# Transposing q by DMA in f16 halves instead of by TensorE in float32

## The chip, the cores and the metric

The kernel runs on one core of a Trainium2 chip. The metric is the device time of one execution in microseconds, the median of several runs. Where runs are compared, the kernel before and the changed one run on the same chip.

## The reference

Eight batches of eight heads, 576 tokens, head size 64: a linear attention, and a feed-forward layer on its output.

```python
# q, k, v: [8, 8, 576, 64] float32; w_in [512, 2048], w_out [2048, 512]
q_s = exp(q - max(q, -1));  q_s = q_s / (sum(q_s, -1) + 1e-9)
k_s = exp(k - max(k, 2));   k_s = k_s / (sum(k_s, 2) + 1e-9)
kv  = einsum('bhsd,bhse->bhde', k_s, v)
x   = einsum('bhsd,bhde->bhse', q_s, kv)     # heads side by side: [4608, 512]
h   = x @ w_in
g   = h * erf(softplus(h))
out = g @ w_out                              # [4608, 512] float32
```

## The kernel before

The feed-forward layer runs over twelve blocks of 384 tokens (three to a pair of batches), each in four groups of 512 hidden columns: 48 items, n = 0 to 47. From item 4 on, matmuls are in f16 with each float32 operand split into a high and a low half, and three products stand for one (high by high, high by low, low by high). For item n, `mm1(n, k)` makes the hidden values in the PSUM banks pX, pY and pZ (a scheme with seven products of halves, k = 0 to 3; groups of twelve matmuls, L905); ScalarE and VectorE copy and add them into the tile H (L917 to L932). `softplus` and `erf` run on ScalarE (L337 is their line, through the helper `act`, and with each goes a table load), `gmul` multiplies on VectorE (L984), and L997 and L1001 split the result into halves. `mm2` multiplies them by w_out into the bank o (L1029, twelve matmuls a group, one group for each 128 tokens), VectorE scales o into ob (L1045), and SP stores it (L1048).

Beside that runs the attention of the batches to come, in the generator `attention(b)`: the k maximum over tokens (`k_max`, L490 to L494, then transposed), q minus its row maximum (L447, L448), exponentials, `kv_mm` and `kv_norm` (kvf is the normalised kv in float32), `kv_split` (from a maximum over all of kv, transposed into x_bk at L119, a scale; then the halves of kv into kvbd, L588 and L589), `q_norm`. Then q, which lies with tokens in rows, is transposed: for a column block c (two heads), `q_cols` puts four transposes of 128 x 128 float32 on TensorE (L610) into a bank qT, and `q_evac` casts it to f16 on ScalarE (L603) and subtracts on VectorE (L604). `x_mm` (L625) makes x from the halves qTs and kvbd, and ScalarE puts it into the blocks of x (L436). The first 512 tokens of a batch are in two tiles q of four heads each (hf = 0, 1; columns 0, 1 and 2, 3); the last 64 of an even batch and its odd partner share the tile qt, transposed (L684) with the odd batch, before the four columns, into qTt and multiplied into xt. Batches 0 and 1 are in float32 throughout.

What sets the order: `pace` takes steps of the generator as the items go on, by the numbers in SHARES, and a scheduler then places every instruction on its engine's queue in that order of priority, as it takes the operands to be ready. Each engine works through its queue in order and waits where an operand isn't there. SP issues the loads and stores in the same way, one queue for all.

The tiles named qT (two buffers) hold the transposed halves; the same two buffers serve `k_max` and kvf.

Of the kernel before, what the change touches and what calls it, by code (L numbers as in the profile page):

```python
# [8 lines left out]
F16 = mybir.dt.float16  # L9
F32 = mybir.dt.float32  # L10
# [3 lines left out]
ALU = mybir.AluOpType  # L14
# [39 lines left out]
def attn_moe_kernel(  # L54
# [15 lines left out]
    TM = 4  # L70
# [26 lines left out]
    vbuf = cp.tile([P, 4, TM, D + 1], F32, name="vbuf")  # L97
    nc.gpsimd.memset(vbuf[:, :, :, D:], 1.0)
    vtail = cp.tile([P, H, D + 1], F32, name="vtail")

    kvbd = []
    for i in range(2):
# [338 lines left out]
    def rows(t):  # L441
        return t.rearrange("p t h d -> p (t h) d")
# [41 lines left out]

    def k_max(b, ks, kt):

        kmax = at.tile([P, H, D], F32, tag="qT", name=f"kmax_{b}")
        k2 = at.tile([P, 2, 4, D], F32, tag="qT", name=f"k2_{b}")
        for hf in range(2):
            nc.vector.tensor_tensor(k2, ks[hf][:, 0:2], ks[hf][:, 2:4], op=ALU.max)  # L490
            nc.vector.tensor_tensor(
                kmax[:, hf * 4:hf * 4 + 4, :], k2[:, 0], k2[:, 1], op=ALU.max
            )
        nc.vector.tensor_tensor(kmax[kt[1]], kmax[kt[1]], kt[0], op=ALU.max)  # L494
        return kmax
# [51 lines left out]
    def kv_norm(b, hf, bk):  # L547
        if b >= E32:
            if hf == 0:
                bat[b]["kvf"] = at.tile([P, NC4, D], F32, tag="qT", name=f"kvf_{b}")  # L550
            kvf = bat[b]["kvf"]
        bkv = bk[:, :2 * W].rearrange("p (c w) -> p c w", c=2)
        rd = at.tile([P, 2, 1], F32, tag="rd", bufs=1, name=f"rd_{b}_{hf}")
        nc.vector.tensor_scalar_add(rd, bkv[:, :, D:], 1e-9)
        nc.vector.reciprocal(rd, rd)
        cs = slice(2 * hf, 2 * hf + 2)
        if b >= E32:
            nc.vector.tensor_tensor(
                kvf[:, cs, :], bkv[:, :, :D], rd.to_broadcast([P, 2, D]), op=ALU.mult
            )  # L560
            return
        for a in range(2):
            ps = slice(a * D, (a + 1) * D)
            nc.vector.tensor_tensor(
                kv32[b][ps, cs, ps], bkv[ps, :, :D], rd[ps].to_broadcast([D, 2, D]),
                op=ALU.mult,
            )
# [25 lines left out]
        if b > 1:  # L593
            nc.vector.tensor_scalar_mul(d["U"], w_u["in"], d["ux"])

    def q_evac(b, bk, name):

        if b < E32:
            qT = at.tile([P, SM], F32, tag="qT", name=name)
            nc.scalar.copy(qT, bk)  # L600
            return qT[:, None, :]
        qT = at.tile([P, 2, SM], F16, tag="qT", name=name)
        nc.scalar.copy(qT[:, 0], bk)  # L603
        nc.vector.tensor_tensor(qT[:, 1], bk, qT[:, 0], op=ALU.subtract)  # L604
        return qT

    def q_cols(b, c, bk):
        hf, c2 = divmod(c, 2)
# [5 lines left out]

    def q_T(b, c, bk):
        q_cols(b, c, bk)
        return q_evac(b, bk, f"qTs_{b}_{c}")

    def x_mm(b, c, out_, qT):

# [15 lines left out]
    def attention(b):  # L636
        d, j, p = bat[b], b % 2, b // 2
        even = bat[b - j]
        tl = slice(j * TAIL, (j + 1) * TAIL)
        ks, qs, kt = d["k"], d["q"], even["kt"][tl]  # L640
        kmax = k_max(b, ks, (kt, tl))
        yield SHARES[0]
        km = k_max_T(b, kmax)
        q_sub(rows(qs[0]), 16, f"q_{b}_0")
        yield SHARES[1]
        kb = k_max_rows(b, km)
        for hf in range(2):
            nc.vector.tensor_tensor(
                ks[hf], ks[hf],
                kb[:, None, hf * 4:hf * 4 + 4, :].to_broadcast([P, TM, 4, D]),  # L650
                op=ALU.subtract,
            )
        nc.vector.tensor_tensor(kt, kt, kb[tl], op=ALU.subtract)
        yield SHARES[2]
        q_sub(rows(qs[1]), 16, f"q_{b}_1")
        if j == 1:
            q_sub(even["qt"], H, f"qt_{p}")
        yield SHARES[3]
        for t in (*ks, kt, qs[0], qs[1], *([even["qt"]] if j == 1 else [])):
            act(t, t, AF.Exp, chain=b > 1)  # L660
        yield SHARES[4]
        kv_norm(b, 0, kv_mm(b, 0))
        d["v"].append(load_half(v, "v", b, 1))
        q_norm(rows(qs[0]), 16, f"q_{b}_0", b)
        yield SHARES[5]
        kv_norm(b, 1, kv_mm(b, 1))
        if b + 1 < B:
            load_kv(b + 1)
        mx = kv_max(b)
        yield SHARES[6]  # L670
        kv_split(b, mx)
        yield SHARES[7]
        q_norm(rows(qs[1]), 16, f"q_{b}_1", b)
        if j == 1:
            q_norm(even["qt"], H, f"qt_{p}", b)
        yield SHARES[8]
        for i in ((3 * p + 1, 3 * p + 2) if j else (3 * p, 3 * p + 1)):
            while not x_free(i):
                yield 0
        if j == 1:  # L680
            qt2 = hd(even["qt"])
            bk = bank(f"qTt_{p}")
            for c in range(NC4):
                nc.tensor.transpose(  # L684
                    bk[:, c * P:(c + 1) * P], qt2[:, c * P:(c + 1) * P], ident
                )
            qT = q_evac(b, bk, f"qTt_{p}")
            if b + 1 < B:
                even_next = bat[b + 1]
                even_next["qt"] = load_tail(q, "qt", p + 1)  # L690
            yield SHARES[9]
            bk = bank(f"xt_{p}")
            x = xblock(p * NBK + 1)
            bk3 = bk.rearrange("p (c s) -> p c s", c=NC4)
            for a in range(2):
                for c in range(NC4):
                    cs = slice(c * P + a * TAIL, c * P + (a + 1) * TAIL)
                    x_mm(2 * p + a, c, bk[:, cs], qT[:, :, cs])
            for a in range(2 if b < E32 else 1):
                w = TAIL if b < E32 else P  # L700
                o = SM - T + a * TAIL
                x_put(
                    bk3[:, :, a * TAIL:a * TAIL + w], x[:, :, o:o + w],
                    bat[a]["sx"] if b < E32 else None,
                )
            yield SHARES[10]
        for c in range(NC4):
            hf, c2 = divmod(c, 2)
            qT = q_T(b, c, bank(f"qT_{b}_{c}"))
            if c2 == 1 and b + 1 < B:  # L710
                load_q(b + 1, hf)
            yield SHARES[11]
            bk = bank(f"x_{b}_{c}")
            x_mm(b, c, bk, qT)
            x_split(b, c, bk)
            if c == NC4 - 1:
                d["xdone"] = True
            yield SHARES[12]
# [14 lines left out]
    def start():  # L733
# [61 lines left out]
        def tc_(c):  # L795
# [3 lines left out]
            if c < 3:  # L799
                bk = psh.tile([P, 512], F32, tag=f"p{'XYZ'[c]}", name=f"qT_0_{c}")  # L800
                qT = r["qT"][:, c]
            else:
                bk = pso.tile([P, 512], F32, tag="o2", name=f"qT_0_{c}")
                qT = at.tile([P, SM], F32, tag="qT", name=f"qTs_0_{c}")
            q_cols(0, c, bk)
            nc.scalar.copy(qT, bk)
            put(f"t{c}", qT[:, None, :])
# [373 lines left out]
```

## Time and profile before

| | |
|---|---|
| three timed runs | 867.26, 867.32, 868.08 us; median 867.32 |
| span of the profiled execution, first to last instruction | 865.1 us (its own time is not recorded apart from the span) |
| TensorE busy | 823.4 us, 95% |
| VectorE busy | 642.5 us, 74% |
| ScalarE busy | 505.9 us, 58% |
| granted TensorE clock, mean | 0.988 |

Matmuls on TensorE overlap, so their busy time is more than the time between their starts. In the rows below, PE is TensorE, PEld its weight loads, DVE is VectorE, ACT is ScalarE, and L12 is line 12 of the kernel. A row of the timeline gives the start in us from the span's start, the length, the engine, the line, the operation, the tiles, how many instructions are merged in it, and the idle time ahead of it with what ended that. A row of the groups gives the count, busy us, the mean ns of one, and the idle us ahead.

### The profile page before, as it was taken

The page shows a single profiled execution, that of the slowest core. Times are in us where ns is not written, and L with a number is a line of the kernel's source. Part 1 is how long each engine was busy: PE and PEld are TensorE (multiplying, and loading weights), DVE is VectorE, ACT ScalarE, POOL GpSimd, SP SyncE. Part 2 cuts the span into 40 slices and gives each one's busy share as a digit, 9 for nine tenths or more (in the row PEclk, how much of TensorE's full clock was granted, in tenths as well). Part 3 has the DMA queues.
Part 4 walks back from the last instruction along what each step waited for, and adds up shares of the span by engine and source line. Part 5 has one row for each costly group of instructions (what it writes and reads, how often), then busy time and mean ns, then how long its engine had stood idle before and what let it go on. Part 6 is the DMA issues. An engine that isn't in the chain of part 4 may idle for free.

```text
span 865.1 us, 15558 instructions
## 1 busy us (share of the span) xinstructions
PE 823.4 (95%) x6556; PEld 570.3 (66%) x6556; DVE 642.5 (74%) x923; ACT 505.9 (58%) x646; POOL 18.2 (2%) x37
## 2 busy tenths in 40 slices
PE   3999996889999999999999999999999999999997
PEld 2655555557766677767776677776776677677672
DVE  6999799899887778858866778867865656653543
ACT  2697677576584567466655467466655456453532
POOL 2101100000000000000000000000000000000000
PEclk9999998889999999999999999999999999999999
DMA  9976730041223202311141212311010000000100
GB/s 270 402 166 184 187 86 1 1 104 26 61 50 80 65 23 50 80 38 25 33 103 32 56 30 50 80 38 25 20 43 2 24 15 1 37 2 1 37 2 37
DMA packets 117381, 55.53 MB, mean 64 GB/s; under 512 B 106560, under 2 KB 108608, under 8 KB 117312
## 3 DMA queue, kind: packets, MB, share of 16 engines
q1 hardware_dynamic: 115136, 46.15, 20.3%
q0 software_dynamic: 2176, 8.39, 2.7%
q8 instruction: 51, 0.84, 0.4%
q14 instruction: 18, 0.15, 0.0%
HBM read 45.09 MB, written 9.44 MB: 63 GB/s over the span
## 4 chain that ended last, share of the span: by engine, by line
PE 73%; DVE 13%; ACT 6%; SPq 3%; DMA 2%; issue 2%; POOL 0%; ACTq 0%; DVEq 0%
PE o L1029 33%; PE pX L905 17%; PE pZ L905 8%; PE pY L905 4%; PE kv L535 3%; ACT L337 2%; ACT G L337 2%; SPq L402 2%; DVE wt L290 2%; PE o L1020 2%; DVE G L984 2%; PE x L625 2%; PE qT L610 1%; DVE H L1001 1%; DMA q<-in_q_dram 1%
## 5 line engine op out<-in xcount | busy, mean ns | idle before, releaser
L1029 PE MATMUL o<-wt,H 128*128 128x512 f16 x1584 | 366.9, 380 | 3.6 <-DVE H L997 3.1
L905 PEld LDWEIGHTS <-wt 128*128 128x128 f16 x3696 | 312.4, 99 | 37.5 <-issue 15.2
L1029 PEld LDWEIGHTS <-H 128*128 128x128 f16 x1584 | 152.4, 98 | 159.0 <-DVE H L997 4.1
L905 PE MATMUL pX<-x,wt 128*128 128x192 f16 x2112 | 208.0, 249 | 9.8 <-ACT H L924 5.7
L337 ACT ACT_TABLE_LOAD x105 | 134.7, 1283 | 7.9 <-DVE H L930 5.7
L984 DVE SCALAR_TENSOR_TENSOR G<-G,small,H 128x1536 f32<-128x1536 f32 x44 | 80.0, 1817 | 65.9 <-ACT G L337 65.8
L905 PE MATMUL pZ<-x,wt 128*128 128x192 f16 x1056 | 103.4, 247 | 0.0
L932 ACT COPY H<-pX 128x384 f32<-128x384 f32 x44 | 20.9, 476 | 139.7 <-PE pX L905 134.7
L337 ACT ACTIVATE G<-H,U 128x768 f32<-128x768 f32 (+1 forms) x60 | 72.8, 1231 | 22.1 <-DVE H L930 21.5
L1001 DVE TENSOR_TENSOR H<-G,H 128x1536 f16<-128x1536 f32 x44 | 77.3, 1756 | 1.1
L337 ACT ACTIVATE G<-G 128x1536 f32<-128x1536 f32 x48 | 71.2, 1484 | 0.5
L905 PE MATMUL pY<-x,wt 128*128 128x192 f16 x528 | 51.1, 246 | 0.5 <-DVE H L917 0.5
L436 ACT ACTIVATE x<-x 128x384 f32<-128x384 f32 (+1 forms) x52 | 17.6, 386 | 56.4 <-PE x L625 54.0
L917 DVE COPY H<-pY 128x384 f32<-128x384 f32 x44 | 24.4, 555 | 30.1 <-PE pY L905 30.1
L997 DVE CAST H<-G 128x1536 f16<-128x1536 f32 x44 | 42.0, 955 | 0.7
L290 DVE SCALAR_TENSOR_TENSOR x<-x,x 128x768 f16<-128x768 f32 (+1 forms) x44 | 37.2, 850 | 5.7 <-ACT x L289 5.6
L289 ACT ACTIVATE x<-x 128x768 f16<-128x768 f32 (+1 forms) x44 | 33.1, 762 | 12.2 <-DVE x L381 12.1
L1045 DVE TENSOR_SCALAR ob<-o,V 128x512 f32<-128x512 f32 x29 | 21.7, 749 | 23.9 <-PE o L1029 23.7
L930 DVE TENSOR_TENSOR H<-pZ,H 128x384 f32<-128x384 f32 x44 | 24.2, 551 | 19.3 <-PE pZ L905 19.3
L919 DVE TENSOR_TENSOR H<-pX,H 128x384 f32<-128x384 f32 x44 | 24.4, 555 | 15.3 <-PE pX L905 14.9
L535 PE MATMUL kv<-vbuf,k 128*64 128x65 f32 x480 | 22.0, 237 | 7.6 <-ACT k L337 5.2
L535 PEld LDWEIGHTS kv<-vbuf,k 128*64 128x64 f32 x480 | 18.7, 149 | 14.5 <-ACT k L337 6.4
(162 smaller groups left out, 823.1 us busy)
## 6 DMA issues: line engine op xcount, KB each, us to landing
out_dram<-ob SPq DMA_DIRECT2D x32, 256.0 KB, 2.2
vbuf<-in_v_dram SPq DMA_DIRECT2D x60, 128.0 KB, 3.0
q<-in_q_dram SPq DMA_DIRECT2D x56, 128.0 KB, 3.0
k<-in_k_dram SPq DMA_DIRECT2D x56, 128.0 KB, 3.3
wt<-in_moe_w_out_dram POOLq DMA_DIRECT2D x5, 1024.0 KB, 6.5
wt<-in_moe_w_in_dram SPq DMA_DIRECT2D x4, 1024.0 KB, 10.7
raw<-in_moe_w_in_dram SPq DMA_DIRECT2D x2, 1024.0 KB, 14.3
wt<-in_moe_w_out_dram SPq DMA_DIRECT2D x2, 1024.0 KB, 16.0
```

The lines of the kernel that those rows point to most:

```text
L289: nc.scalar.activation(hi, src, AF.Copy, scale=s)
L290: nc.vector.scalar_tensor_tensor(lo, src, s, hi, op0=ALU.mult, op1=ALU.subtract)
L337: i = nc.scalar.activation(out_, in_, func, **kw)
L535: nc.tensor.matmul(bk[a * D:(a + 1) * D, c * W:(c + 1) * W], kk, vv, start=(t == 0), stop=(t == TM),)
L905: nc.tensor.matmul(o, w[wl][:, c, a * P:(a + 1) * P], x[:, xl, xi, c, :], start=(new and a == 0 and c == 0 and i == 0), stop=(c == 1 and i ...
L917: nc.vector.tensor_copy(C[0, 0], bank2("Y"))
L919: add(C[0, 0], bank2("X"), C[0, 0], op=ALU.add)
L930: add(C[0, 1], bank2("Z"), C[0, 1], op=ALU.add)
L984: nc.vector.scalar_tensor_tensor(flat(s["G"]), flat(s["G"]), GA[:, g:g + 1], flat(s["H"]), op0=ALU.mult, op1=ALU.mult,)
L997: nc.vector.tensor_copy(flat(s["gh"]), flat(s["G"]))
L1001: nc.vector.tensor_tensor(flat(s["gl"]), flat(s["G"]), flat(s["gh"]), op=ALU.subtract)
L1029: nc.tensor.matmul(o, s[gt][:, a, ts_], w[wl][:, a, :], start=(first_ and a == 0 and i == 0), stop=(last_ and a == FG - 1 and i == 2),)
```

## The change

For batches 2 to 7 the halves are made while q still has tokens in rows: ScalarE casts a whole tile q of 128 x 1024 to f16, VectorE subtracts, both into a scratch tile, and one DMA transpose, issued by SP, puts all sixteen blocks of 128 x 128 into the place where q was. For qt it is eight blocks. `x_mm` reads its operand there. Since q's place is in use until `x_mm` has read it, the loads of the next batch's q and qt stand behind the x products. A single scratch tile asc takes the place of the two buffers named qT: it holds the halves on their way, the k maximum, kvf, and for batches 0 and 1 the transposed q.

```diff
+    asc = cp.tile([P, 2, 512], F32, name="asc")
+    qhl = asc.rearrange("p h n -> p (h n)").bitcast(F16)
...
-        kmax = at.tile([P, H, D], F32, tag="qT", name=f"kmax_{b}")
-        k2 = at.tile([P, 2, 4, D], F32, tag="qT", name=f"k2_{b}")
+        kmax = asc[:, 0].rearrange("p (h d) -> p h d", h=H)
+        k2 = asc[:, 1].rearrange("p (t h d) -> p t h d", t=2, h=4)
...
-                bat[b]["kvf"] = at.tile([P, NC4, D], F32, tag="qT", name=f"kvf_{b}")
+                bat[b]["kvf"] = asc[:, 0, :NC4 * D].rearrange("p (c e) -> p c e", c=NC4)
...
+    def q_halves(q_, n):
+
+        hl = [qhl[:, i * n:(i + 1) * n] for i in range(2)]
+        nc.scalar.copy(hl[0], q_)
+        nc.vector.tensor_tensor(hl[1], q_, hl[0], op=ALU.subtract)
+
+
+    def q_turn(q_, n):
+
+        q_halves(q_, n)
+        t = q_.bitcast(F16).rearrange("p (n s) -> p n s", s=P)
+        nc.sync.dma_start_transpose(t, qhl[:, :2 * n])
+        return t
+
+    def q_turn_half(b, hf):
+        t = q_turn(bat[b]["q"][hf].rearrange("p t h d -> p (t h d)"), TM * 4 * D)
+        t = t.rearrange("p (i t c) s -> p i c t s", i=2, t=TM)
+        for c in range(2):
+            bat[b].setdefault("qT", {})[2 * hf + c] = t[:, :, c]
...
         kv_split(b, mx)
         yield SHARES[7]
+        if b >= E32:
+            q_turn_half(b, 0)
         q_norm(rows(qs[1]), 16, f"q_{b}_1", b)
...
         yield SHARES[8]
+        if b >= E32:
+            q_turn_half(b, 1)
...
+            if b >= E32:
+                qT = q_turn(qt2, H * D).rearrange("p (i c) s -> p i (c s)", i=2)
...
-            if b + 1 < B:
-                even_next = bat[b + 1]
-                even_next["qt"] = load_tail(q, "qt", p + 1)
             yield SHARES[9]
...
+            if b + 1 < B:
+                bat[b + 1]["qt"] = load_tail(q, "qt", p + 1)
             yield SHARES[10]
         for c in range(NC4):
             hf, c2 = divmod(c, 2)
-            qT = q_T(b, c, bank(f"qT_{b}_{c}"))
-            if c2 == 1 and b + 1 < B:
-                load_q(b + 1, hf)
+            qT = q_T(b, c, bank(f"qT_{b}_{c}")) if b < E32 else d["qT"][c]
             yield SHARES[11]
             bk = bank(f"x_{b}_{c}")
             x_mm(b, c, bk, qT)
+            if c2 == 1 and b + 1 < B:
+                load_q(b + 1, hf)
             x_split(b, c, bk)
```

How this moves the instructions, at two places. The first is ScalarE around the tail of batch 5, in items 23 and 24. Before, the casts of the transposed tail (qTt_2) and of column 0 stand behind the copies of item 23:

```order
L922 COPY H_23_4382<-pZ_23_4451 128x2x192
L924 COPY H_23_4382<-pX_23_4397 128x2x192
L603 CAST qTt_2_4496<-qTt_2_4491 128x512
L436 ACTIVATE x_7_3523<-xt_2_4502 128x4x128
L603 CAST qTs_5_0_4558<-qT_5_0_4553 128x512
L932 COPY H_23_4382<-pX_23_4397 128x2x192
L289 ACTIVATE x7_7_4970<-x_7_3523 128x768
L337 ACT_TABLE_LOAD
L337 ACTIVATE G_23_4587<-H_23_4382,U_3_2321 128x1536
```

Now (lines are those of the changed kernel: L604 is the cast in `q_halves`, L944 to L954 are the copies of H, L342 softplus and erf):

```order
L944 COPY H_23_4278<-pZ_23_4350 128x2x192
L946 COPY H_23_4278<-pX_23_4293 128x2x192
L604 CAST asc_88<-q_5_0_3501 128x1024
L954 COPY H_23_4278<-pX_23_4293 128x2x192
L342 ACT_TABLE_LOAD
L342 ACTIVATE G_23_4476<-H_23_4278,U_3_2280 128x1536
L604 CAST asc_88<-q_5_1_3682 128x1024
L342 ACT_TABLE_LOAD
L342 ACTIVATE G_23_4476<-G_23_4476 128x1536
L944 COPY H_24_4480<-pZ_24_4529 128x2x192
L946 COPY H_24_4480<-pX_24_4495 128x2x192
L604 CAST asc_88<-qt_2_2399 128x512
```

Three casts stand where two stood, all into asc; the second lies between softplus and erf of item 23, the third behind the copies of item 24, and the tail's x (xt_2) comes a part of an item later than before.

The second place is VectorE in batch 4, items 17 and 18. Before, the subtractions of columns 1 and 2 stand among the steps of G and H, and the q maximum of batch 5 follows:

```order
L984 SCALAR_TENSOR_TENSOR G_17_3464<-G_17_3464,small_84,H_17_3290 128x1536
L604 TENSOR_TENSOR qTs_4_1_3530<-qT_4_1_3525,qTs_4_1_3530 128x512
L997 CAST H_17_3290<-G_17_3464 128x1536
L1001 TENSOR_TENSOR H_17_3290<-G_17_3464,H_17_3290 128x1536
L447 TENSOR_REDUCE q_5_0_m_3942<-q_5_0_3533 128x16
L448 TENSOR_TENSOR q_5_0_3533<-q_5_0_3533,q_5_0_m_3942 128x1024
L927 TENSOR_TENSOR H_18_3469<-pX_18_3484,H_18_3469 128x2x192
```

Now (L605 is the subtraction in `q_halves`, L495 to L499 the k maximum, L452 the q maximum):

```order
L1006 SCALAR_TENSOR_TENSOR G_17_3387<-G_17_3387,small_84,H_17_3215 128x1536
L605 TENSOR_TENSOR asc_88<-q_4_1_2641,asc_88 128x1024
L1019 CAST H_17_3215<-G_17_3387 128x1536
L1023 TENSOR_TENSOR H_17_3215<-G_17_3387,H_17_3215 128x1536
L949 TENSOR_TENSOR H_18_3392<-pX_18_3407,H_18_3392 128x2x192
L495 TENSOR_TENSOR asc_88<-k_5_0_3165 128x512
L496 TENSOR_TENSOR asc_88<-asc_88 128x256
L495 TENSOR_TENSOR asc_88<-k_5_1_3170 128x512
L496 TENSOR_TENSOR asc_88<-asc_88 128x256
L499 TENSOR_TENSOR asc_88<-asc_88,kt_2_2227 64x512
L952 TENSOR_TENSOR H_18_3392<-pZ_18_3448,H_18_3392 128x2x192
L452 TENSOR_REDUCE q_5_0_m_3839<-q_5_0_3501 128x16
```

The whole second half is subtracted in one instruction, and the k maximum of batch 5, which writes the same scratch tile, has moved ahead of its q maximum.

More of the change, by code (lines that the diff above doesn't have):

```diff
@@ L594, in kv_split @@
             nc.vector.tensor_scalar_mul(d["U"], w_u["in"], d["ux"])
[L596 to L605, printed above, removed]
+    def q_halves(q_, n):
[12 more added lines that the diff above has]
+            bat[b].setdefault("qT", {})[2 * hf + c] = t[:, :, c]
     def q_cols(b, c, bk):
@@ L616, in q_T @@
         q_cols(b, c, bk)
-        return q_evac(b, bk, f"qTs_{b}_{c}")
+        nc.scalar.copy(asc[:, c % 2], bk)
+        return asc[:, None, c % 2]
     def x_mm(b, c, out_, qT):
@@ L681, in attention @@
             qt2 = hd(even["qt"])
[L682 to L687, printed above, removed]
-            if b + 1 < B:
-                even_next = bat[b + 1]
-                even_next["qt"] = load_tail(q, "qt", p + 1)
+            if b >= E32:
+                qT = q_turn(qt2, H * D).rearrange("p (i c) s -> p i (c s)", i=2)
+            else:
+                bk = bank(f"qTt_{p}")
+                for c in range(NC4):
+                    nc.tensor.transpose(
+                        bk[:, c * P:(c + 1) * P], qt2[:, c * P:(c + 1) * P], ident
+                    )
+                nc.scalar.copy(asc[:, 0], bk)
+                qT = asc[:, None, 0]
             yield SHARES[9]
@@ L803, in tc_ @@
                 bk = pso.tile([P, 512], F32, tag="o2", name=f"qT_0_{c}")
-                qT = at.tile([P, SM], F32, tag="qT", name=f"qTs_0_{c}")
+                qT = asc[:, 0]
             q_cols(0, c, bk)
```

## The prediction

> **What bounds the kernel now.** I read the page first: its span, the busy slices, then busy time by stretch (the windows view, columns PE, PEld, DVE, ACT, POOL busy, granted clock, DMA share).
>
> ```profile
> span 865.1 us, 15558 instructions
> PE   3999996889999999999999999999999999999997
> 330.00:480.00 150.00, 148.90 (x1329) 106.29 (x1327) 112.44 (x172) 87.24 (x106) 1.26 (x4) 1.00 0.23 54
> 480.00:690.00 210.00, 208.91 (x1825) 150.21 (x1824) 153.88 (x222) 123.14 (x152) 0.63 (x2) 1.00 0.14 35
> ```
>
> From 330 to 690 us, where batches 4 to 7 are prepared, TensorE is busy 357.8 of 360 us at full clock; VectorE has about a quarter free, ScalarE over 40%. So TensorE's order is the clock: what leaves it is won, and whatever it waits for is lost, since nothing behind it can catch up. DMA is at 14 to 23%: bandwidth is no limit, only how long one transfer takes.
>
> **The change, priced.** Groups by line and shape (count, busy us, mean ns, idle before and its releaser):
>
> ```profile
> L610 PE MATMUL qT<-ident,q 128*128 128x128 f32 x128 | 20.0, 283 | 0.0
> L625 PE MATMUL xt<-qTt,kvbd 128*128 128x64 f16 x72 | 3.1, 192 | 3.4 <-DVE qTt L604 2.1 <-ACT qTt L603 1.3
> L603 ACT CAST qTs<-qT 128x512 f16<-128x512 f32 x24 | 14.1, 588 | 19.1 <-PE qT L610 19.1
> L604 DVE TENSOR_TENSOR qTs<-qT,qTs 128x512 f16<-128x512 f32 x24 | 16.5, 686 | 9.1 <-ACT qTs L603 9.1
> L448 DVE TENSOR_TENSOR q<-q,q_m 128x1024 f32<-128x1024 f32 x14 | 17.0, 1218 | 0.1
> L447 DVE TENSOR_REDUCE q_m<-q 128x16 f32<-128x1024 f32 x14 | 17.0, 1213 | 2.5 <-DMA q<-in_q_dram 2.4
> L337 ACT ACTIVATE q<-q 128x1024 f32<-128x1024 f32 x14 | 14.2, 1048 | 0.4 <-DVE q L448 0.3
> ```
>
> Matmuls overlap, so a mean of 283 ns isn't what one costs TensorE. That is the distance between starts, here around batch 4 (timeline of TensorE: start, length, instructions):
>
> ```profile
> 361.19 0.27 PE L119 MATMUL x_bk<-ident,mx 128*128 128x128 f32 x1
> 361.30 0.60 PE L610 MATMUL qT<-ident,q 128*128 128x128 f32 x4
> 361.74 1.15 PE L905 MATMUL pX<-x,wt 128*128 128x192 f16 x12
> 371.87 0.81 PE L625 MATMUL x<-qTs,kvbd 128*128 128x512 f16 x3
> ```
>
> Four transposes take 0.44 us. Removed are 24 such groups (six batches) and 3 of the tails: 27 x 0.44 = 11.9 us. With them go the 3.4 us that xt waits for the tail's halves. Gain: 15.3 us, all on the path.
>
> Casts and subtractions: twelve casts of 128x1024 at about 1.05 us (nearest the Exp of that size, 1048 ns) and three of 0.59 replace 27 of 588 ns (14.4 for 15.9 us); twelve subtractions at about 1.22 (L448's size) and three of 0.69 replace 27 of 686 ns (16.7 for 18.5 us). Both engines have room, so I count nothing; but their place matters. Each half has to be cast, subtracted and turned by a DMA that SP issues, before x may read it. All halves use one scratch tile, so the next cast on ScalarE, and the next batch's k maximum on VectorE, wait until the DMA has read it: cast, subtract, turn, one after the other, two times in an even batch and three in an odd one.
>
> No row shows a DMA transpose. Call its time from VectorE's last write to the released wait D for a half (512 KB of f16), Dt for a tail (256 KB). The nearest rows (issues with KB each and median us to landing; the line with three numbers is of the first two 512 KB loads):
>
> ```profile
> DMA to landing us min/median/max: 4.1/4.8/5.5
> G_raw<-in_q_dram SPq DMA_DIRECT2D x1, 512.0 KB, 7.2
> out_dram<-ob SPq DMA_DIRECT2D x32, 256.0 KB, 2.2
> q<-in_q_dram SPq DMA_DIRECT2D x56, 128.0 KB, 3.0
> q1 hardware_dynamic: 115136, 46.15, 20.3%
> ```
>
> Lower bound 2.2 us (a 256 KB store). Upper: packets took 0.203 x 16 x 865.1 us / 115136 = 24.4 ns each; cut into pieces of 32 bytes a half is 16384 packets, 25 us on 16 engines. Equal size speaks for 4.1 (the first load, alone) to 7.2 us (a later one among others); I take the middle, D = 5.6, and Dt = 3.9, on the line from 3.0 at 128 KB to D at 512 KB (so Dt follows D below).
>
> *Batches 4 and 6.* VectorE there (same columns):
>
> ```profile
> 366.47 0.99 DVE L589 SCALAR_TENSOR_TENSOR kvbd<-kvf,x_s,kvbd 64x256 f16<-64x256 f32 x2
> 367.50 0.75 DVE L1045 TENSOR_SCALAR ob<-o,V 128x512 f32<-128x512 f32 x1
> 368.16 0.55 DVE L930 TENSOR_TENSOR H<-pZ,H 128x384 f32<-128x384 f32 x1
> ```
>
> The cast of half 0 must wait for L589, since kvf now lies in the same scratch: it ends at 367.46, or 366.9 with L604's 0.6 us gone from ahead of it. Cast to 367.9; VectorE has ob and L930 to 368.1, then the subtraction to 369.3; the half is there at 369.3 + D. In the new order TensorE comes to x of column 0 at 371.87 less one group, 371.4. It waits D - 2.1 = 3.5 us. Half 1 is cast behind erf and x of column 2 stands some 16 us behind x of column 0 in the new order: hidden. Two batches: 7.0 us.
>
> *Batches 5 and 7.* TensorE, VectorE and ScalarE around batch 5:
>
> ```profile
> 453.19 0.27 PE L119 MATMUL x_bk<-ident,mx 128*128 128x128 f32 x1
> 453.30 1.15 PE L905 MATMUL pZ<-x,wt 128*128 128x192 f16 x12
> 454.29 1.15 PE L905 MATMUL pX<-x,wt 128*128 128x192 f16 x12
> 455.28 2.75 PE L1029 MATMUL o<-wt,H 128*128 128x512 f16 x12
> 457.87 0.60 PE L684 MATMUL qTt<-ident,qt 128*128 128x128 f32 x4
> 460.30 0.48 DVE L589 SCALAR_TENSOR_TENSOR kvbd<-kvf,x_s,kvbd 64x256 f16<-64x256 f32 x1
> 461.43 0.55 DVE L927 TENSOR_TENSOR H<-pX,H 128x384 f32<-128x384 f32 x1
> 466.58 0.48 ACT L932 COPY H<-pX 128x384 f32<-128x384 f32 x1 [1.40 <-PE pX L905]
> 469.11 1.58 ACT L337 ACTIVATE G<-H,U 128x1536 f32<-128x1536 f32 x1
> 470.70 1.28 ACT L337 ACT_TABLE_LOAD   x1
> 472.00 1.49 ACT L337 ACTIVATE G<-G 128x1536 f32<-128x1536 f32 x1
> ```
>
> Between starts a group of twelve takes TensorE 0.99 us (pX, pY, pZ: call it f1) or 2.59 us (o). In the new order x_bk is followed by ten f1 groups, four o groups and eleven products of a fifth, and then by xt: 453.3 + 9.9 + 10.36 + 2.37 = 475.9. The chain starts at 460.8, when kvf is free: cast to 461.9; L927 (0.55) and two small scales, subtraction to 463.1; turned at 463.1 + D. ScalarE meanwhile copies (0.48, from 463.6, when TensorE has done the third pX), loads a table (1.28) and runs softplus (1.58) to 467.0, so the second cast waits for D above 3.9. It ends at 464.2 + D (1.1 us), its subtraction at 465.4 + D, the turn at 465.4 + 2D. Then the tail: cast 0.6, subtraction 0.7, turn Dt: 466.7 + 2D + Dt. TensorE waits 2D + Dt - 9.25 = 5.85 us. Two batches: 11.7 us. (Of this, from D = 4.7 on, a part shows earlier, where erf, behind the second cast, holds the copy that frees bank pX.)
>
> *Batches 3 and 2.* The same, with these anchors:
>
> ```profile
> 206.59 1.81 DVE L984 SCALAR_TENSOR_TENSOR G<-G,small,H 128x1536 f32<-128x1536 f32 x1
> 214.35 0.81 PE L625 MATMUL x<-qTs,kvbd 128*128 128x512 f16 x3
> 265.57 0.27 PE L119 MATMUL x_bk<-ident,mx 128*128 128x128 f32 x1
> 267.80 0.99 DVE L589 SCALAR_TENSOR_TENSOR kvbd<-kvf,x_s,kvbd 64x256 f16<-64x256 f32 x2
> ```
>
> Batch 3: cast from 268.8, subtraction to 271.5; on ScalarE the second cast stands behind table, softplus, table, erf and two copies, 269.9 + 6.6 = 276.5, so D up to 5.0 is covered; the tail's turn ends at 275.2 + 2D + Dt against xt at 284.1, again counted by groups: 2D + Dt - 8.9 = 6.2 us (D + Dt - 3.9 for D under 5). Batch 2: the first subtraction follows L984, ending at 209.6; x of column 0 now stands behind o groups that ended at 214.35 before, 211.5 without the two x and two qT groups and a batch start 0.4 earlier: D - 1.9. The second half waits for the first: cast and subtraction 2.3 us, another D, against 5.3 us of TensorE's work after x: D - 3.0. Together 2D - 4.9 = 6.3 us.
>
> Sum: 7.0 + 11.7 + 6.2 + 6.3 - 15.3 = +15.9 us on the profiled span, 865.1 to 881.0. The runs' median, 867.32, holds 2.2 us around that span, taken as unchanged: 883.
>
> SP's queue: the turns stand ahead of the next batch's q loads, which now also follow x of every second column instead of its transposes, some 5 us later. Their first reader, the q maximum on VectorE, then holds back the copies behind it; I take nothing, since TensorE comes to those 3.5 us later itself, and at most 2 us a batch if a turn holds SP for longer than a plain issue.
>
> The Trainium skill (VectorE: DVE Perf Modes, section The three transpose paths) has a rule against this change: a 128x128 transpose of two-byte values takes 390 ns by TensorE and 1309 ns by DMA. By that, sixteen in a row are an estimated 20.9 us for a half, the far end of rival 3, and the sum would be about +190 us. The trace has TensorE's transpose of four-byte values at 0.11 us of its path and the DMA's not at all.
>
> **The rivals.**
> 1. *The turn is quick and hidden.* It decides below D = 4.1. For it: the store's 2.2 us, and DMA engines four fifths idle. Against: each of the 512 KB rows took longer. At D = 2.2, Dt = 2.2 batches 2 and 4 to 7 wait under 1 us each and batch 3 1.6, 3.4 in all: -11.9, 855.4.
> 2. *Gain and waits cancel.* With the first load's 4.1 and Dt = 3.4 the waits are 3.3 + 3.6 + 4.0 + 4.6 = 15.5: 867.5. The Trainium skill (DMA: Bandwidth & Descriptors, section Latency and other measured facts) gives DMA transposes 261 GB/s; an estimate from it, 2.0 us for a half above a short transfer's landing, comes out here too; no row shows that rate.
> 3. *The turn is cut small.* For it: 24.4 ns a packet, whatever its size may be; against: nothing in the trace transposes. At D = 10, Dt = 5.3: 15.1 + 16.4 + 15.8 + 32.1 = 79.4 of waits, +64: 931. At 25 us it would be over 1100.
>
> **How the numbers follow.** Likeliest, D from 4.4 to 8: 0.50, 870 to 910 by the same formulas, 883 at my D. Rival 1: 0.25, 855 to 865. Rival 2: 0.07. Rival 3, D above 8: 0.18. A change under 0.2% (1.7 us) can't be told from none here. So slower 0.68, same 0.07, faster 0.25. The range 855 to 920 leaves out what lies above D = 8.9, at most 0.15, and little else.
>
> **What would show it.** Right: new idle on TensorE before xt and x, released by DMA or by VectorE's subtraction; ScalarE waiting before the second cast; no qT group in batches 2 to 7; DMA transposes landing in 4.4 to 8 us. Wrong: landing under 4 us and TensorE's slices still full through 200 to 690 us, or a landing over 8 us. If SP issues a turn for several us, the q maximum's wait of 2.4 us grows instead.

## The result, and the profile after

The changed kernel takes 874.54 us (median of 4 runs, 873.36 to 875.39) against 867.5 (4 runs on the same chip, 867.26 to 868.08): a ratio of 1.0085, with a 95% interval from 1.007 to 1.0099. So it is slower, by about 7 us. The forecast had the direction and, in its range, the time, but its +15.9 us was more than twice what came. The profiled execution took 874.55 us, 1.85 us around its span.

The page and the windows view of the changed kernel, the same lines as before (busy PE, PEld, DVE, ACT, POOL, then granted clock and DMA share):

```profile
span 872.7 us, 15341 instructions
PE   3999996898999899999999899999999899999997
PEclk9999998799999899999999999999999999999999
330.00:480.00 150.00, 148.00 (x1312) 105.42 (x1310) 113.40 (x168) 88.52 (x103) 1.26 (x4) 1.00 0.28 64
480.00:690.00 210.00, 200.48 (x1761) 142.05 (x1760) 154.37 (x219) 120.01 (x145) 0.63 (x2) 1.00 0.22 49
```

From 480 to 690 us TensorE was idle for 1.1 us before and is now for 9.5. The last four 8s of the busy slices (196, 283, 480 and 676 us; a slice is 21.8 us) are where x of batches 2, 3, 5 and 7 is made; the second also has an 8 in the clock. What TensorE waits for stands in the groups by line and shape (count, busy, mean ns, idle ahead and what ended it), and for L612, the DMA transposes, in the view of one line (issue time on SP's queue in ns, minimum, median and maximum, first and last start, then the time to landing):

```profile
L640 PE MATMUL x<-q,kvbd 128*128 128x512 f16 x72 | 19.9, 389 | 5.9 <-DMA q<-asc 5.9
L640 PE MATMUL xt<-qt,kvbd 128*128 128x64 f16 x72 | 3.2, 209 | 8.4 <-DMA qt<-asc 8.4
L604 ACT CAST asc<-q 128x1024 f16<-128x1024 f32 x12 | 12.5, 1042 | 34.8 <-DVE kvbd L594 25.6 <-DMA q<-asc 9.2
L604 ACT CAST asc<-qt 128x512 f16<-128x512 f32 x3 | 1.9, 617 | 9.8 <-DMA q<-asc 9.8
L605 DVE TENSOR_TENSOR asc<-q,asc 128x1024 f16<-128x1024 f32 x12 | 14.7, 1221 | 9.7 <-ACT asc L604 9.7
L452 DVE TENSOR_REDUCE q_m<-q 128x16 f32<-128x1024 f32 x14 | 17.0, 1213 | 6.9 <-DMA q<-in_q_dram 6.8
L612 SPq DMA_TRANSPOSE q<-asc x12: 1779/1940/2885, 210.8 to 674.0; - x12
L612 SPq DMA_TRANSPOSE qt<-asc x3: 1232/1232/1233, 286.7 to 679.7; - x3
DMA to landing us min/median/max: 3.0/4.3/6.1
```

Of the marks that the forecast named, all but the landing time are there: no group of transposes in batches 2 to 7, new idle time before xt (8.4 us) and x (5.9), released by the DMA, ScalarE waiting before the casts, and a q maximum that waits longer (6.8 us for 2.4). The casts and subtractions cost what was priced (1042 and 617 ns, 1221 ns). The landing is smaller than priced: 4.3 us in the median for a half, just under the 4.4 to 8 us named, and 3.0 us for a tail.

Batch 5 shows the chain, all engines in order of time:

```profile
466.46 0.48 DVE L594 SCALAR_TENSOR_TENSOR kvbd<-asc,x_s,kvbd 64x256 f16<-64x256 f32 x1
466.98 1.05 ACT L604 CAST asc<-q 128x1024 f16<-128x1024 f32 x1 [4.86 <-DVE kvbd L594]
468.06 1.23 DVE L605 TENSOR_TENSOR asc<-q,asc 128x1024 f16<-128x1024 f32 x1 [0.22 <-ACT asc L604]
473.97 1.04 ACT L604 CAST asc<-q 128x1024 f16<-128x1024 f32 x1 [0.81 <-DMA q<-asc]
475.05 1.23 DVE L605 TENSOR_TENSOR asc<-q,asc 128x1024 f16<-128x1024 f32 x1 [2.72 <-ACT asc L604]
480.62 0.62 ACT L604 CAST asc<-qt 128x512 f16<-128x512 f32 x1 [2.06 <-DMA q<-asc]
481.27 0.69 DVE L605 TENSOR_TENSOR asc<-qt,asc 128x512 f16<-128x512 f32 x1 [0.61 <-ACT asc L604]
485.05 0.86 PE L640 MATMUL xt<-qt,kvbd 128*128 128x64 f16 x24 [2.79 <-DMA qt<-asc]
```

The first cast waits for kv's split (L594), the second for the transpose of half 0, the third for that of half 1, and xt for the tail's. From the end of a subtraction to the next row of the chain: 469.29 to 473.97, 476.28 to 480.62 and 481.96 to 485.05, that is 4.68, 4.34 and 3.09 us.

### The profile page after: what moved, and what is told of

Same layout as the page of the kernel before. It is cut to its first block, busy times and chain, and to the rows that moved or that the text cites. A ratio compares the mean times of both kernels' runs of the same rounds, so it can differ in the third digit from the quotient of the medians.

```text
span 872.7 us, 15341 instructions
## 1 busy us (share of the span) xinstructions
PE 815.5 (93%) x6448; PEld 558.6 (64%) x6448; DVE 642.5 (74%) x911; ACT 506.0 (58%) x634; POOL 18.1 (2%) x37
## 4 chain that ended last, share of the span: by engine, by line
PE 60%; DVE 21%; DMA 10%; ACT 5%; issue 3%; SPq 2%; POOL 0%; ACTq 0%; DVEq 0%; POOLq 0%
PE o L1051 28%; PE pX L927 15%; PE pZ L927 8%; DMA q<-asc 5%; PE pY L927 3%; PE kv L540 2%; DVE wt L295 2%; ACT G L342 2%; DVE G L1006 2%; PE x L640 2%; ACT L342 2%; DVE H L1023 1%; DVE asc L605 1%; SPq L407 1%; DMA wt<-in_moe_w_out_dram 1%
## 5 line engine op out<-in xcount | busy, mean ns | idle before, releaser
L1006 DVE SCALAR_TENSOR_TENSOR G<-G,small,H 128x1536 f32<-128x1536 f32 x44 | 79.9, 1815 | 49.4 <-ACT G L342 49.3
L954 ACT COPY H<-pX 128x384 f32<-128x384 f32 x44 | 20.9, 475 | 138.7 <-PE pX L927 133.8
L342 ACT ACTIVATE G<-H,U 128x768 f32<-128x768 f32 (+1 forms) x60 | 72.8, 1231 | 22.1 <-DVE H L952 21.5
L342 ACT ACTIVATE G<-G 128x1536 f32<-128x1536 f32 x48 | 71.2, 1484 | 0.5
L441 ACT ACTIVATE x<-x 128x384 f32<-128x384 f32 (+1 forms) x52 | 17.4, 387 | 42.4 <-PE x L640 39.9
L1067 DVE TENSOR_SCALAR ob<-o,V 128x512 f32<-128x512 f32 x29 | 21.7, 748 | 26.5 <-PE o L1051 26.4
L941 DVE TENSOR_TENSOR H<-pX,H 128x384 f32<-128x384 f32 x44 | 24.4, 554 | 16.8 <-PE pX L927 16.2
L604 ACT CAST asc<-q 128x1024 f16<-128x1024 f32 x12 | 12.5, 1042 | 34.8 <-DVE kvbd L594 25.6
L949 DVE TENSOR_TENSOR H<-pX,H 128x384 f32<-128x384 f32 x44 | 24.2, 550 | 5.4 <-PE pX L927 5.3
```

What stands on the lines that cost most here:

```text
L342: i = nc.scalar.activation(out_, in_, func, **kw)
L941: add(C[0, 0], bank2("X"), C[0, 0], op=ALU.add)
L949: add(C[1, 1], bank2("X"), C[1, 1], op=ALU.add)
L1006: nc.vector.scalar_tensor_tensor(flat(s["G"]), flat(s["G"]), GA[:, g:g + 1], flat(s["H"]), op0=ALU.mult, op1=ALU.mult,)
```

## The experiments

All times are medians; a ratio is to the kernel before, run on the same chip in the same call. "Lag" is the start of the same o group in two traces, one less the other; it tells where along the program time is lost.

**1. The transposes put back as idle work.** What was the removed TensorE work worth?

```diff
+                idle4(f"qTt_{p}")          # four transposes of ident into a bank, before xt
...
+                qT = d["qT"][c]
+                idle4(f"qT_{b}_{c}")       # and before each x
```

> Edit: the changed kernel, with 27 groups of four float32 transposes put back on TensorE at their old places, of a constant and into a bank that nothing reads; the DMA transposes stay. It measures what the removed TensorE work was worth. By the prediction's 0.44 us a group: 27 x 0.44 = 11.9 us if every group is on the path, 886.4 us; less the groups that stand where TensorE now waits (before xt in three batches, before x in batches 2, 4 and 6: some 6 to 7 groups, 3 us), so 883.5 us is the likeliest. Rival A (the transposes were mostly hidden, so the change had little to gain): 875 to 878 us. Rival B (the work keeps TensorE's clock up where the idle now halves it): 3 us less than the likeliest, 880.5 us.

Measured: 879.34 us, ratio 1.0148 (1.0131 to 1.0165): 4.8 us more than the changed kernel and not 9. In the even batches 4 and 6, where the clock is full in both traces, the lag between the two grows by 1.91 us (items 15 to 20) and 1.98 us (items 27 to 32) for four groups each: 0.48 and 0.50 a group, so the prediction's 0.44 holds there. The difference is made elsewhere. In batch 3 (items 10 to 15) the lag falls by 1.34 us, where five groups should add 2.4: there the changed kernel loses half its clock for a while and this one doesn't (both by window, busy times as above):

```profile
265.00:305.00 40.00, 37.00 (x288) 25.00 (x286) 27.23 (x45) 19.73 (x25) 0.29 (x2) 0.91 0.45 96
265.00:305.00 40.00, 37.00 (x317) 26.63 (x315) 29.03 (x46) 20.89 (x28) 0.00 (x0) 1.00 0.42 92
```

The first row is the changed kernel, with a granted clock of 0.91, the second this one. It has its slow stretches elsewhere (0.72 from 481 to 487 us). The idle work doesn't simply keep the clock up. The other part is scatter. At item 6, ahead of batch 2's x, this trace is already 3.06 us ahead of the changed kernel's; so is the trace of the run with the filler (8), by 3.07 us, and up to there its instructions are in the changed kernel's order. One trace against another can't settle 3 us of the time before item 6.

**2. A plain copy instead of the transpose.** The data aren't transposed; queue, places and bytes are the same.

```diff
-        nc.sync.dma_start_transpose(t, qhl[:, :2 * n])
+        nc.sync.dma_start(t, qhl[:, :2 * n].rearrange("p (n s) -> p n s", s=P))
```

> Edit: the DMA moves the same bytes between the same places as a plain copy; the transposing is left out. It measures what of the landing time is the transposing. Theory A (4.3 us is mostly the transposing): the copy lands in some 2.2 us (the value of the prediction's first rival), all waits before xt and x go with the half clock, 874.5 - 14.3 - 3 = 857 us. Theory B (mostly the queue, the descriptors and the semaphores, alike for both): the copy lands in 4 us or more, 872 to 876 us. Between them each us of landing time is worth up to 10 us until the waits run out.

Measured: 856.49 us, ratio 0.9879 (0.9864 to 0.9894). The waits of this kernel, the issue times and the landing:

```profile
L612 SPq DMA_DIRECT2D q<-asc x12: 498/516/528, 208.5 to 657.1; - x12
DMA to landing us min/median/max: 2.2/3.0/3.9
PE xt L640 <- DMA qt<-asc: 2.1, 3, 0.9
PE x L640 <- DMA q<-asc: 1.0, 3, 0.5
```

The copy lands in 3.0 us, between the two theories, and that is enough: the waits at x and xt fall from 14.3 to 3.1 us, and no stretch of half clock is left from 190 to 720 us. ScalarE's and TensorE's orders are nearly those of the changed kernel, so this is the clean test of the prediction's steepness: 1.3 us less a half and about 0.8 less a tail (481.96 to 485.05 against 470.58 to 472.90 in batch 5) take off 18 us. By its formulas, in which D counts nine times below 5 us and no wait falls below nothing, the waits go from 17.4 us (D = 4.4, Dt = 3.1) to 4.3 (3.0 and 2.3): 13.1 us, plus about 3 for the clock. The 2 us left are no more than this trace is ahead at item 6 (2.29 us), where traces scatter.

Transposing itself costs 1.3 us a half and 1.4 us on SP's queue (1940 for 516 ns). The packets of the queue (count, MB, share of the 16 DMA engines) in the changed kernel, then here; before the change they were 115136:

```profile
q1 hardware_dynamic: 143264, 53.23, 24.3%
q1 hardware_dynamic: 117296, 53.23, 22.8%
```

For the same bytes the transposes add 28128 packets, some 2080 a half, and the copies 2160, or 160 a half. In batch 5 a transposed half is 2048 packets of 256 bytes, 21.7 ns each in the mean, and a copied one 128 packets of 4 KB, 161 ns each, with 32 packets of 4 bytes beside them in both. Spread over 16 engines that is an estimated 2.8 us against 1.3, which fits the 1.3 us between the landings; no run changed the size of the packets alone.

**3. Each turn done twice.**

```diff
-        nc.sync.dma_start_transpose(t, qhl[:, :2 * n])
+        for _ in range(2):
+            nc.sync.dma_start_transpose(t, qhl[:, :2 * n])
```

> Edit: the changed kernel with each turn done twice, the second transpose behind the first with the same source and place, so that the landing time of a turn about doubles (some 8.7 us for a half, 6.1 us for a tail, to be read from the rows). It tests the prediction's formulas for the waits (batches 4, 6: D - 2.1; 5, 7: 2D + Dt - 9.25; 3: 2D + Dt - 8.9; 2: 2D - 4.9). By these the waits are 68.8 us where the changed kernel's 4.4 and 3.1 give 16.8: 52 us more, 874.5 + 52 = 926 us. If a wait in one batch gives the next one's turn a head start, or if later waits are hidden behind others: 900 to 915 us. If SP's queue, held twice as long, delays the loads of q, k and v too: over 935 us.

Measured: 890.51 us, ratio 1.0276 (1.0261 to 1.0292): 16 us more than the changed kernel, not 52, and below all three times expected. The landing did double: in batch 4 the subtraction ends at 377.26 and the next cast starts at 385.91, 8.65 us. But the scheduler, which knows of the second transpose, placed x later. TensorE in batch 4, here and in the changed kernel:

```profile
377.38 2.75 PE L1052 MATMUL o<-wt,H 128*128 128x512 f16 x12
379.97 1.15 PE L928 MATMUL pZ<-x,wt 128*128 128x192 f16 x12
380.96 1.15 PE L928 MATMUL pX<-x,wt 128*128 128x192 f16 x12
381.95 1.03 PE L1052 MATMUL o<-wt,H 128*128 128x512 f16 x4
385.87 0.81 PE L641 MATMUL x<-q,kvbd 128*128 128x512 f16 x3 [2.90 <-DMA q<-asc]
```

```profile
375.28 2.75 PE L1051 MATMUL o<-wt,H 128*128 128x512 f16 x12
379.55 0.81 PE L640 MATMUL x<-q,kvbd 128*128 128x512 f16 x3 [1.51 <-DMA q<-asc]
```

Two groups and a third of one more now stand ahead of x: 2.84 us of work where there was idle time. So the formulas hold only for the order for which they were written; this run can't tell what the changed kernel's order would have cost at D = 8.7.

**4. A scratch of its own for each half.** The other scratch, asc, keeps kvf and the tail.

```diff
+            turn.append(rp.tile([P, 2, 1024], F32, tag="raw", bufs=1, name="turn"))
+        return turn[0][:, slot].bitcast(F16)      # slot 2, the tail: asc as before
```

> Edit: the two halves' f16 parts get a scratch of their own each; the tail keeps the old one. Order of work unchanged. Main theory (the chain through the one scratch sets the tail's arrival: half 1's cast waits for half 0's transpose to have read the scratch, the tail's cast for half 1's): the three waits before xt (8.4 us in all in the profile of the changed kernel) go, and with the first of them the 6.8 us at half clock (about 3 us), so 874.5 - 11.4 = 863 us; the waits at x in batches 4 and 6 (half 0's own landing, about 1.5 us each) stay, and ScalarE's wait before the casts (19.0 us in 6) is gone. Rival A (the three transposes run after each other anyway, in SP's queue or in the transfer, some 4.3 + 4.3 + 3.1 us): the waits before xt stay, 872 to 875 us. Rival B (VectorE is what makes the halves late, not the scratch): xt's wait turns into one on the subtraction, 870 to 874 us.

Measured: 857.24 us (855.58 to 857.51), ratio 0.9885 (0.987 to 0.99): 17.3 us faster than the changed kernel and faster than the one before. But the reason given was not the whole one. Batch 5:

```profile
438.63 1.92 SPq L622 DMA_TRANSPOSE q<-turn  x1
455.08 0.48 DVE L594 SCALAR_TENSOR_TENSOR kvbd<-asc,x_s,kvbd 64x256 f16<-64x256 f32 x1
455.60 0.62 ACT L613 CAST asc<-qt 128x512 f16<-128x512 f32 x1 [4.86 <-DVE kvbd L594]
460.04 0.86 PE L650 MATMUL xt<-qt,kvbd 128*128 128x64 f16 x24 [1.84 <-DMA qt<-asc]
```

The second half's transpose is issued 16 us ahead of kv's split, where it stood behind it. Once the halves don't share a tile with kvf, the scheduler places their casts and subtractions an item earlier. Only the tail still waits for kv's split, and xt for the tail, 1.84 us here and 1.86 in batch 7. The waits at x in the even batches, which the expectation let stay, are gone as well. Two things were changed in one: which tile kvf is in, and how many places the halves have. The next two runs take them apart.

**5. Both halves in one place, apart from kvf.** The diff is `turn[0][:, 0]` for `turn[0][:, slot]`.

> Edit: as the run with a scratch for each half, but both halves use one of the two places, so half 1's cast waits until half 0's transpose has read it; kvf and the tail stay in asc. The order on the engines is that of the run with two places. Theory K: as there, 856 to 858 us, with new waits on ScalarE before the second cast of at most 2 us each that TensorE doesn't see. Theory S: the second turn lands one landing time later and the waits come back, 865 us or more.

Measured: 858.2 us, ratio 0.9896 (0.9876 to 0.9916), not to be told from two places. ScalarE does wait before the second cast, and nobody minds:

```profile
ACT turn L613 <- DMA q<-turn: 9.5, 6, 4.0
```

9.5 us in six times, up to 4.0, more than the 2 expected. So a second place for the halves isn't what counts, once they are apart from kvf and the tail.

**6. kvf out of the scratch, one line.** The halves and the tail still share asc.

```diff
-                bat[b]["kvf"] = asc[:, 0, :NC4 * D].rearrange("p (c e) -> p c e", c=NC4)
+                bat[b]["kvf"] = sqs.bitcast(F32).rearrange("p (c e) -> p c e", c=NC4)
```

> Edit: the changed kernel with one line different: kvf (1 KB a partition) lies in a tile that is free by then, not in the scratch asc. The halves and the tail still share asc. By the instruction order the three turns of a batch now stand ahead of kv's second half instead of behind kv's split. Theory K (kvf in the scratch is what puts the turns behind kv's split, and so the landing onto TensorE's path; the chain through one scratch is harmless if it starts an item earlier): the waits before x and xt go, the tail's too: the run with a scratch for each half gave 857.2 and kept 1.8 us before xt in two batches, so 853 to 855 us. Theory S (the chain of three through one scratch is what costs): the casts still wait for the transpose ahead of them (19.0 us on ScalarE now), that holds erf and the copies behind them, and TensorE waits elsewhere: 865 to 875 us.

Measured: 864.1 us (862.53 to 865.36), ratio 0.9972 (0.996 to 0.9984): 10 us faster than the changed kernel by this one line, but short of the 853 to 855 of theory K, and just outside theory S's range. Both name a part. Batch 5, ScalarE, VectorE and TensorE:

```profile
446.06 0.62 ACT L604 CAST asc<-qt 128x512 f16<-128x512 f32 x1 [5.74 <-DMA q<-asc]
454.74 1.82 DVE L1006 SCALAR_TENSOR_TENSOR G<-G,small,H 128x1536 f32<-128x1536 f32 x1 [2.31 <-ACT G L342]
456.47 0.47 DVE L594 SCALAR_TENSOR_TENSOR kvbd<-sqs,x_s,kvbd 64x256 f16<-64x256 f32 x1
460.56 0.47 PE L640 MATMUL xt<-qt,kvbd 128*128 128x64 f16 x10 [1.61 <-DVE kvbd L594]
```

The transposes are early, even the tail's. But now ScalarE stands 5.74 us before the tail's cast for the transpose of a half, erf behind it comes late, VectorE waits 2.31 us for that at L1006, and the rest of kv's split stands behind L1006: TensorE waits for kvbd before xt. So two halves in one place cost nothing (5). Three pieces in one place do (6), by these rows, though kvf lies in a different tile in the two runs.

**7. Four orders.** The first writes half 0's turn behind its normalization and half 1's ahead of kv's split, with a place for each half:

```diff
         q_norm(rows(qs[0]), 16, f"q_{b}_0", b)
+        if b >= E32:
+            q_turn_half(b, 0)
...
+        q_norm(rows(qs[1]), 16, f"q_{b}_1", b)
+        if b >= E32:
+            q_turn_half(b, 1)
+        yield SHARES[7]
         kv_split(b, mx)
```

> Edit: as the run with a scratch for each half, and the turns are written earlier: half 0's right behind its normalization, ahead of the second half of kv; half 1's normalization and turn ahead of kv's split. Main theory (only the landing time after the last subtraction costs): the waits at x in the even batches (5.9 us in all) go as well as those before xt, 863 - 5.9 = 857 us, and not below 867.5 - 15.3 = 852 us, the time before less the whole gain counted in the prediction. Rival A (kv's split now ends later on VectorE by half 1's normalization and subtraction, and TensorE waits for it before x instead): a wait on VectorE before x of 2 us in six batches, 869 to 875 us. Rival B (SP's queue stands longer at the transposes, so keys, values and q of the next batch land later): the waits for q and k grow by 2 us or more a batch, 870 to 880 us.

Measured: 855.3 us (854.79 to 855.35), ratio 0.9865 (0.9851 to 0.988). The 1.86 and 1.85 us before xt are left. The second adds the tail ahead of kv's split and takes kvf out of asc:

> Edit: a place for each half, kvf out of asc, and all three turns written ahead of kv's split (the tail's too, which stands just before xt otherwise). If only the 1.84 and 1.86 us before xt in batches 5 and 7 are left of the costs (the run with the earlier halves had them and gave 855.3): 851.6 us. Rival A: kv's split, now behind the tail's normalization too, comes late and TensorE waits for it before xt: 855 to 858 us. Rival B: the loads of q come later behind the turns in SP's queue and VectorE's q maximum waits longer (13.6 us in all in the run with the earlier halves against 6.8 in the changed kernel): 855 us.

Measured: 857.78 us, ratio 0.9897 (0.9878 to 0.9917), no gain. The tail's wait is gone, and rival A's is there, 3.69 us, though not for the reason given. VectorE, then TensorE:

```profile
447.29 0.69 DVE L495 TENSOR_TENSOR asc<-k 128x512 f32<-128x512 f32 x1 [3.30 <-DMA k<-in_k_dram]
449.09 0.28 DVE L126 TENSOR_REDUCE x_e<-x_bk 128x1 f32<-128x128 f32 x1
453.94 0.29 PE L650 MATMUL xt<-qt,kvbd 128*128 128x64 f16 x2 [3.69 <-DVE kvbd L593]
```

VectorE stands for 3.30 us at the next batch's k maximum, for a k that is still being loaded, with the scale of kv behind it. The third writes half 1 behind kv's split and the tail ahead of it, to see whether half 1's work mattered:

> Edit: half 0 turned early in its own place, then the tail (in asc, with kvf elsewhere), then kv's split, then half 1. It tells whether the wait for kv's split in the run before came from half 1's work ahead of it on VectorE or from the next batch's k maximum, which may start early once kvf has left asc. If from half 1's: no wait before xt, 851 to 853 us. If from the k maximum (three to four operations of VectorE then stand ahead of kv's split): the wait for kv's split of 2 to 4 us in one or two batches stays, 856 to 859 us.

Measured: 858.72 us, ratio 0.9912 (0.9895 to 0.9928), with 4.28 us before xt for kv's split. The scheduler placed half 1's subtraction ahead of kv's split all the same, so it did not isolate that; but VectorE again stood 4.7 us at L495 for a k. So in a fourth, kvf stays in asc, which keeps the k maximum behind, and the tail uses half 0's place, long free by then:

```diff
-        return turn[0][:, slot].bitcast(F16)
+        return turn[0][:, slot % 2].bitcast(F16)  # the tail, slot 2, uses place 0; kvf stays in asc
```

> Edit: as the run with the earlier halves, and the tail's normalization and turn also ahead of kv's split, its f16 halves in the place of half 0, which has long been turned by then; kvf stays in asc, so that the next batch's k maximum cannot come ahead of kv's split on VectorE. If the 1.86 and 1.85 us before xt in batches 5 and 7 go and kv's split comes at most 0.7 us (one subtraction of 128x512) later: 855.3 - 3.7 = 851.6 us, at best. If VectorE is then late with kv's split, as in the run that also took kvf out of asc (3.7 us before xt in batch 5): 855 to 858 us.

Measured: 855.19 us (852.96 to 856.52), ratio 0.9864 (0.9843 to 0.9885). No engine waits for a transpose any more; before xt stay 0.87 us in batches 5 and 7, for kv's split. It beats the kernel before by 1.4%, and can't be told from the run with the earlier halves.

**8. Work in place of the idle time.** Does the idle time before xt halve the clock?

```diff
+            for _ in range(10 if b >= E32 else 0):
+                nc.tensor.matmul(bk, ident.bitcast(F16)[:, :P], qhl[:, :512], start=True, stop=True)
```

> Edit: the changed kernel with ten f16 matmuls of 128x512 into the bank xt just ahead of xt in batches 3, 5 and 7, about 2.2 us of work that nothing uses, where TensorE now waits 2.6 to 3.0 us for the tail's transpose. If that idle time is what halved the clock for 6.8 us in batch 3: no half clock there, some 3 us less, 871.5 us. If the half clock comes at other times and for other reasons: 874 to 875 us. If the filler itself holds up xt because it waits with the scratch: up to 876 us.

Measured: 878.29 us, ratio 1.0135 (1.012 to 1.015), 3.8 us slower than the changed kernel and above the 876 us expected at most. The filler reads the scratch, so TensorE waited for the tail's cast ahead of it:

```profile
477.93 4.43 PE L716 MATMUL xt<-asc,ident 128*128 128x512 f16 x10 [2.44 <-ACT asc L604]
```

2.44 us idle, and then ten matmuls at half clock, 4.43 us where they took 2.32 in batch 3 (there after 2.35 us idle). It moved the idle time instead of filling it; the question was not answered by it, but by the rows of all runs together (last section).

## Why the prediction was wrong

**The landing time was mis-sized.** The step that failed is "I take the middle, D = 5.6, and Dt = 3.9". Measured, the first halves land 4.3 to 4.7 us after the subtraction, with one at 6.1 (batch 7), the second ones 4.3 to 4.4 in the odd batches, and the tails 3.1: D was 4.4 in the median, the lowest value of its likeliest range. The lone first load's 4.1 us was the better neighbour than the 7.2 of a load among others, as DMA is at 22 to 28% in this part of the program. With ten D (nine below 5 us) and three Dt in the sum, that takes 11.8 us off the waits.

| us | b2 | b3 | b4 | b5 | b6 | b7 | sum |
|---|---|---|---|---|---|---|---|
| forecast, D = 5.6, Dt = 3.9 | 6.3 | 6.2 | 3.5 | 5.85 | 3.5 | 5.85 | 31.2 |
| same formulas, landing as measured | 4.15 | 3.5 | 2.3 | 2.9 | 2.2 | 4.35 | 19.4 |
| idle before x and xt | 2.9 | 2.6 | 1.5 | 2.8 | 1.45 | 3.0 | 14.3 |
| idle before pX for a copy behind the casts | | 0.4 | 0.5 | | 0.5 | 1.1 | 2.5 |

The second row is worked out from the subtractions' ends and the next rows, as shown for batch 5: 4.68 + 4.34 + 3.09 - 9.25 = 2.9; batch 3 goes by the form for D under 5 us, 4.33 + 3.11 - 3.9. The row is 2.6 us above the third and fourth together, half of that in batch 2. The remark that part of the wait shows earlier, at bank pX, came true (1.13 us in batch 7). With the measured landing the sum would have been 19.4 - 15.3 = +4.1.

**The idle time was priced at its own length.** In batch 3 it cost more. TensorE of the changed kernel:

```profile
289.82 1.44 PE L640 MATMUL xt<-qt,kvbd 128*128 128x64 f16 x24 [2.58 <-DMA qt<-asc]
291.07 1.47 PE L640 MATMUL x<-q,kvbd 128*128 128x512 f16 x3
292.98 4.11 PE L1051 MATMUL o<-wt,H 128*128 128x512 f16 x12
```

x takes 1.47 us for 0.81, and o 4.11 for 2.75: 6.8 us at half clock, 3.4 us of work lost (an estimate, half of its length). No term of the sum had that.

**Late q loads took something.** "I take nothing" was short by 1.3 us: the q maximum waited 2.05 us for its load at 314.48, VectorE's copies behind it came late, and pX waited 0.61 us at 323.48 and 0.67 at 519.78.

**The gain was right**, 0.48 and 0.50 us a group in experiment 1 for 0.44. Together: 14.3 + 2.5 of waits, 1.3 for the loads, 3.4 for the clock, less 11.9 and 3.4, are +6.2 against 7.6 on the two spans. By item, batches 3 to 7 come out to 0.3 us each. The 1.4 us left lies ahead of item 8, where the lag to the kernel before is 2.53 us and batch 2's waits less its four groups are 1.14. The filler's trace of experiment 8, with the same order of instructions up to there, is 3.15 us ahead of the changed kernel's at that item, so 1.4 us can't be told from scatter.

**The sign was partly luck.** The waits that the sum is about, 14.3 + 2.5, less the gain of 15.3 are +1.5 us, within the 1.7 us that the prediction couldn't tell from none. That the change is slower by clearly more is owed to the half clock and the late loads, which the sum didn't have.

**The rivals.** Rival 2 (D = 4.1, gain and waits cancel) was nearest in its size of D, and got 7 of 100. Rival 1's waits are 1.0 us by the prediction's own formulas and not 3.4 (batch 3 is then D + Dt - 3.9 = 0.5), so it stood for 853 us, below the range. Rival 3's price of a packet was near, 24.4 ns for 21.7, but the pieces have 256 bytes and not 32: 2048 a half and not 16384. The Trainium skill (VectorE: DVE Perf Modes, section The three transpose paths) spoke against the change with 1309 ns for a block of 128x128 by DMA; added up, that would be 20.9 us for a half. The trace shows sixteen blocks in 4.3 us, 0.27 us each, so times of single blocks can't be added. What was right in it is the sign at this order of work.

**What the forecast didn't see** is that its own anchor, "the cast of half 0 must wait for L589, since kvf now lies in the same scratch", was the cause to look at. It priced the chain from there on and not the sharing that put it there. One line takes 10 us off (experiment 6), one place for the halves apart from kvf and the tail 16 (5), and the landing time, still 4.4 to 4.5 us in the median there, is mostly hidden.

## What to carry to other kernels

When a new tile takes over several old uses, ask for each pair what now waits for what, and what a scheduler that orders by readiness will move because of it: here 1 KB a partition of kvf in the scratch placed all transposes of a batch behind kv's split, and taking it out let the next batch's k maximum slip ahead. A new transfer's time was better taken here from a lone one of its size, with the DMA engines mostly idle, and its coefficient in the sum (ten here) says how much a wrong guess costs. Moving work from TensorE to DMA paid 1.4% once its results were started an item ahead of their use.

## What the hardware showed

A DMA transpose of 512 KB of f16 within SBUF lands in 4.3 us and goes in 2048 packets of 256 bytes, one of 256 KB lands in 3.0 us, where a plain copy of 512 KB takes 3.0 with 128 packets; its issue holds SP's queue for 1.9 us (1.2 for 256 KB) against 0.5.

The clock: over the traces of all thirteen kernels, from 190 us to TensorE's last matmul, idle times of TensorE of 1.4 to 1.9 us were never followed by a half clock (17 of 17), those of 3.67 us and more always (6 of 6), and those of 1.94 to 3.0 us in 8 of 15 (2.03 in experiment 1 was, 3.00 was not). No half clock stood there without such an idle time ahead of it.

What decides in between is where the idle time lies. In each trace the half clocks start on a grid of 3.413 us, in the changed kernel at 142.12, 155.77 and 288.89 us, 4 and 39 steps apart. By steps of this grid, with what follows the first (busy times as above, batch 3 and batch 7):

```profile
285.48:288.89 3.41, 1.34 (x15) 1.05 (x13) 2.15 (x4) 2.51 (x4) 0.00 (x0) 1.00 0.30 58
288.89:295.72 6.83, 5.90 (x38) 3.29 (x38) 2.78 (x5) 4.95 (x6) 0.00 (x0) 0.50 0.24 51
678.01:681.42 3.41, 1.78 (x9) 0.69 (x7) 2.77 (x4) 0.62 (x1) 0.00 (x0) 1.00 0.17 34
681.42:684.83 3.41, 2.06 (x31) 1.34 (x31) 0.35 (x1) 1.13 (x2) 0.00 (x0) 1.00 0.23 43
```

In batch 3 TensorE was idle for 2.07 us of one step, and the clock was halved from its end. The 2.99 us before xt in batch 7 fell on two steps, 1.63 and 1.35 us, and no half clock followed. Over all traces, every step at full clock with 2.02 us or more of idle time was followed by a half clock (13 of 13), one of five with 1.85 to 1.90 us was, and none with less.

The Trainium skill (TensorE: Matmul & The Clock Gate, section Part 1: The HAM clock gate) tells of a free-running window of about 3.4 us that has to be idle. The grid agrees with the window, but here 2.0 us of idle time in it were enough. The advice of its section Why this matters for your kernels, to keep gaps under about 3 us, is too wide here: 1.95 us was once enough. That the idle time causes the stretch rests on these counts; no run changed one idle time and nothing else.
